# First batch of an attention and MLP kernel reordered: f32 staging of first heads, constants in two parts, PE transposes for the second batch, W1 ahead of most of W2

## Chip, cores, metric

One NeuronCore of a Trainium2 chip. The metric is device time of one execution in microseconds (us); most executions of one kernel agree to about 0.3%. Engines: PE = TensorE, DVE = VectorE, ACT = ScalarE, POOL = GpSimd, SP = SyncE. The clock of PE is read in two ways: the granted clock is a column of the profile, and the spacing of like matmuls shows the speed at which they ran.

## The reference

Grouped attention (8 batches, 16 q heads on 4 k/v heads, 384 positions, head size 64), then a residual MLP with an affine token mixer:

```python
scores = q @ k.T / sqrt(D);  attn = softmax(scores);  x = attn @ v   # x: [8, 384, 1024]
a1 = alpha1 * x + beta1
tok = einsum('ts,bsd->btd', w_tok, a1)
u = x + lam * tok
a2 = alpha2 * u + beta2
out = u + lam * (relu(a2 @ w_ch1) @ w_ch2)      # w_ch1: [1024, 4096], w_ch2: [4096, 1024]
```

Inputs are f32; the kernel works in bf16 and casts in the DMA where it can. W1 (w_ch1) does not stay on chip: each batch streams it again, 16 chunks through a ring of four. W2 stays.

## The kernel before

A batch has a side part (attention, tok, a2) and a main part (h = W1 product, ch = W2 product). The side part of batch b+1 is a list of small units that are interleaved with the matmuls of main(b). Batch 0 has no main part to hide behind: its side part is the prologue. A unit works on a pair of heads, p. A flip is a transpose; ident is the identity matrix with which PE transposes. The constants are alpha1 (g1), beta1 (h1), lam, alpha2 (al2) and beta2 (be2), spread over all partitions; "the chain" is DVE's work from its first reciprocal (softmax of the first pair) to the start of h.

```python
def load_q(b, i=0, n=Hq):              # cast to bf16 by POOL's DMA, pieces of one head row
    ...
    nc.gpsimd.dma_start(out=qrs[b][:, st, i:i + n], in_=by_st(q[b])[:, st, i:i + n])
...
def av_piece(p, hh):                   # one head of pair p
    ...                                # 9 matmuls
    if hh == 0:
        if p == 0 and first:           # constants folded once, whole width
            nc.vector.tensor_tensor(out=g1, in0=g1, in1=lam_t, op=MUL)
            nc.vector.tensor_tensor(out=h1, in0=h1, in1=lam_t, op=MUL)
        return
    ...                                # rinv, x (L205, L208), a1f = x * g1 (L211), a1 = a1f + h1 (L214)
def tok(p):
    ...                                # 9 matmuls; u (L224), a2f = u * al2 (L226), a2 = a2f + be2 (L229)
def a2_transpose(p):
    if not first:
        nc.sync.dma_start_transpose(...)   # batches 1 to 7
        return
    ...                                    # batch 0: PE and an ACT copy
...
# main(b), after W1 chunk c
load_w1(b * NCH + c + RING)
if b == 0 and c < 12:
    load_w2(1, c, NNT)
if b == 0 and c == 12:
    for i in range(3, 8):
        load_w2(1, i, 8)
...
# the program
load_k(0); load_q(0, 0, 8); make_identity(nc, ident)
... place_k(0); load_v(0); wtok_in; load_q(0, 8, 8)
for c in range(RING):
    load_w1(c)
load_w2(0, 0, 1)                       # the whole first half of W2, 4 MB in bf16
for i, f in enumerate(side(0)):
    f()
    ...                                # constants on ACT's queue after units 2 and 4, load_k(1) after 5
load_q(1); place_k(1); load_v(1); flip_k(1); flip_q(1)      # flips: DMA transposes
for b in range(B):
    us = side(b + 1) if b + 1 < B else []
    lead = 0.2 if b == 0 else 0.0
    for dt in main(b):                 # yields every 4 matmuls
        t += dt
        if done < len(us) and done * t_all * (0.95 - lead) < len(us) * (t - t_all * lead):
            us[done](); done += 1
```

The softmax here doesn't subtract the row's maximum and nothing guards it: scores larger than these inputs give would overflow.

## Time and profile before

| | us |
|---|---|
| time, median of 4 runs | 843.5 (842.17 to 843.87) |
| prologue, up to the first h matmul | 52.7 |
| batch 0 (h 61.4, ch 49.9) | 111.3 |
| batches 1 to 6, each | 98.1 |
| batch 7 (nothing beside it) and tail | 85.0 and 5.1 |

A stage begins at its first matmul.

### The profile page before, as it was taken

The numbers are of one execution on the slowest core, as the hardware profiler recorded it, in microseconds if no ns is written. First come the engines' busy times: TensorE is split into PE (matmuls) and PEld (weight loads), VectorE is DVE, ScalarE is ACT, GpSimd is POOL, SyncE is SP. The second block draws the span as 40 slices with busy tenths as digits, with TensorE's granted clock in tenths as the row PEclk, the third lists the DMA queues.
The fourth block names the chain that finished last, engine by engine and source line by source line (L and its number), as shares of the span: only waits on it lengthen the run. The fifth ranks groups of instructions, "written<-read, shape, count | busy, mean of one in ns | idle before, by whom it ended". The sixth has DMA issues, their size and how long they took to land.

```text
span 842.7 us, 13619 instructions
## 1 busy us (share of the span) xinstructions
PE 805.2 (96%) x5765; PEld 432.8 (51%) x5765; DVE 362.7 (43%) x737; ACT 210.7 (25%) x331; POOL 199.6 (24%) x246
## 2 busy tenths in 40 slices
PE   4776999999999999999999999999999999999997
PEld 2443544555545554555545554455545555455543
DVE  1741445534453444624445444544445345451111
ACT  5511432143113331043221331133320432101100
POOL 6473450022401232022500224012410221003100
PEclk9779999999999999999999999999999999999999
DMA  9999999699927999499975999279995999129811
GB/s 209 220 163 194 199 201 168 125 163 179 140 63 139 172 181 97 107 140 177 163 70 122 168 176 136 70 138 171 178 96 109 123 174 149 35 52 182 113 37 38
DMA packets 272045, 116.66 MB, mean 138 GB/s; under 512 B 121712, under 2 KB 265072, under 8 KB 271984
## 3 DMA queue, kind: packets, MB, share of 16 engines
q0 software_dynamic: 204000, 83.67, 86.5%
q1 hardware_dynamic: 67264, 29.50, 16.1%
q10 hardware_dynamic: 720, 2.62, 0.8%
q8 instruction: 45, 0.74, 0.3%
q14 instruction: 16, 0.13, 0.1%
HBM read 173.08 MB, written 12.58 MB: 220 GB/s over the span
## 4 chain that ended last, share of the span: by engine, by line
PE 88%; DMA 7%; DVE 3%; ACT 1%; issue 1%; POOL 0%; ACTq 0%; DVEq 0%; POOLq 0%
PE ch L331 40%; PE h L311 37%; DMA w<-in_moe_w_ch_dram 5%; PE sc L178 4%; PE av L196 4%; PE tok L221 4%; DMA h<-in_moe_beta_dram 1%; DMA q_raw<-in_q_dram 1%; DVE a2f L226 1%; DVE x L208 1%; DVE a1f L211 1%; ACT hT L316 0%; DVE x L224 0%; POOL q_raw L101 0%; DVE qT L170 0%
## 5 line engine op out<-in xcount | busy, mean ns | idle before, releaser
L311 PE MATMUL h<-a2T,w 128*128 128x384 bf16 x2048 | 361.6, 329 | 9.9 <-DMA w<-in_moe_w_ch_dram 9.0
L331 PE MATMUL ch<-w,hT 128*128 128x512 bf16 x1536 | 353.1, 379 | 0.0
L311 PEld LDWEIGHTS <-w 128*128 128x128 bf16 x2048 | 191.5, 98 | 149.7 <-issue 21.3
L125 POOL DMA_DIRECT2D w<-in_moe_w_ch_dram x128 | 112.4, 880 | 555.8 <-PE sc L178 273.3
L181 ACT ACTIVATE es<-sc 128x768 bf16<-128x768 f32 x192 | 145.3, 810 | 340.8 <-PE sc L178 340.6
L331 PEld LDWEIGHTS <-hT 128*128 128x128 bf16 x1536 | 142.3, 98 | 160.7 <-issue 9.2
L318 DVE TENSOR_SCALAR hT<-h 128x384 bf16<-128x384 f32 x128 | 71.2, 556 | 193.7 <-PE h L311 193.7
L316 ACT ACTIVATE hT<-h 128x384 bf16<-128x384 f32 x128 | 62.9, 492 | 233.4 <-PE h L311 233.4
L336 DVE TENSOR_TENSOR o<-ch,lam 128x512 f32<-128x512 f32 x48 | 33.1, 689 | 115.1 <-PE ch L331 115.1
L224 DVE TENSOR_TENSOR x<-tok,x 128x384 f32<-128x384 f32 x64 | 35.6, 556 | 80.5 <-PE tok L221 80.5
L196 PEld LDWEIGHTS <-es 128*128 128x128 bf16 x1152 | 52.5, 99 | 27.7 <-issue 6.5
L196 PE MATMUL av<-v,es 128*128 128x65 bf16 x1152 | 57.4, 195 | 4.5 <-DVE x L208 4.1
L178 PE MATMUL sc<-qT,kT 64*128 64x384 bf16 x384 | 51.7, 340 | 2.2 <-ACT es L181 1.3
L221 PE MATMUL tok<-a,wtokT 128*128 128x128 bf16 x576 | 44.2, 223 | 5.3 <-POOL a L214 2.8
L221 PEld LDWEIGHTS <-wtokT 128*128 128x128 bf16 x576 | 38.4, 100 | 16.9 <-issue 3.5
L208 DVE TENSOR_TENSOR x<-av,rinv 128x192 f32<-128x192 f32 x128 | 39.8, 352 | 2.2
L226 DVE TENSOR_TENSOR a2f<-x,al 128x384 f32<-128x384 f32 x64 | 37.4, 585 | 2.7
L211 DVE TENSOR_TENSOR a1f<-x,g 128x384 f32<-128x384 f32 x64 | 36.2, 566 | 2.7
L205 DVE RECIPROCAL rinv<-av 128x6 f32<-128x6 f32 x64 | 12.2, 191 | 55.7 <-PE av L196 55.7
L337 DVE TENSOR_TENSOR o<-o,x 128x512 f32<-128x512 f32 x48 | 33.2, 692 | 1.6
L229 DVE TENSOR_TENSOR a<-a2f,be 128x384 bf16<-128x384 f32 x57 | 31.8, 558 | 2.0
L214 DVE TENSOR_TENSOR a<-a1f,h 128x384 bf16<-128x384 f32 x57 | 31.8, 558 | 2.0
(32 smaller groups left out, 130.6 us busy)
## 6 DMA issues: line engine op xcount, KB each, us to landing
w<-in_moe_w_ch_dram POOLq DMA_DIRECT2D x133, 512.0 KB, 6.9
out_dram<-o SPq DMA_DIRECT2D x48, 256.0 KB, 2.2
q_raw<-in_q_dram POOLq DMA_DIRECT2D x21, 256.0 KB, 8.0
w<-in_moe_w_ch_dram POOLq DMA_DIRECT2D x1, 4096.0 KB, 39.8
kst<-in_k_dram SPq DMA_DIRECT2D x16, 192.0 KB, 3.1
v<-in_v_dram POOLq DMA_DIRECT2D x24, 64.0 KB, 7.8
w<-in_moe_w_ch_dram POOLq DMA_DIRECT2D x12, 128.0 KB, 9.9
a2T<-a SPq DMA_TRANSPOSE x56, 3.8
```

The source lines that it names most:

```text
L125: nc.gpsimd.dma_start(out=t, in_=w1src[:, :, c * CW * P:(c + 1) * CW * P])
L178: nc.tensor.matmul(out=sc[:, hh, :S].rearrange("p (st s) -> p st s", st=NST), lhsT=kT[r, sk, hk, :], rhs=qT[r, :, p, :], start=True, stop= ...
L181: nc.scalar.activation(out=e, in_=sc[:, :, :S], func=EXP, scale=scale_qk)
L196: nc.tensor.matmul(out=av[:, hh, sq, :], lhsT=ess[p, sk][:, hh, sq * P:(sq + 1) * P], rhs=vb[:, sk, hk, :], start=(sk == 0), stop=(sk == N ...
L208: nc.vector.tensor_tensor(out=x[:, :, c0:c0 + D], in0=av[:, hh, :, :D], in1=rinv[:, hh].to_broadcast([P, NST, D]), op=MUL)
L211: nc.vector.tensor_tensor(out=t, in0=x[:, :, cols(p)], in1=bc(g1, p), op=MUL)
L221: nc.tensor.matmul(out=ps[:, tt, :], lhsT=wtokT[:, st, tt * P:(tt + 1) * P], rhs=a1s[p][:, st, :], start=(st == 0), stop=(st == NST - 1))
L226: nc.vector.tensor_tensor(out=t, in0=u, in1=bc(al2, p), op=MUL)
L311: nc.tensor.matmul(out=ps[:, :S], lhsT=w1[:, dt, j * P:(j + 1) * P], rhs=a2T[:, dt, :], start=(dt == 0), stop=(dt == NDT - 1))
L316: nc.scalar.activation(out=hT[:, nt, :], in_=ps[:, :S], func=RELU)
L318: nc.vector.tensor_scalar_max(out=hT[:, nt, :], in0=ps[:, :S], scalar1=0.0)
L331: nc.tensor.matmul(out=ps, lhsT=hT[:, nt, ms * P:(ms + 1) * P], rhs=w2[:, nt, cs], start=(nt == 0), stop=(nt == NNT - 1))
```

## The change

Its intent is to shorten the prologue and to keep PE supplied in batch 0. Its parts: (1) k in separate halves, the first four q heads staged in f32 rows over ACT's queue, nine warming matmuls; (2) the constants in two column parts on two queues, issued early; (3) q, k and v of batch 1 loaded within the prologue; (4) PE transposes for k, q and a2 of batch 1, and DMA transposes for five of the eight a2 of batch 0; (5) half as much of W2 ahead of h, the rest between the chunks of W1; (6) batch 1's side work packed into h of batch 0.

```diff
+        pe_flip = b < 2
@@ av_piece
-                if p == 0 and first:
-                    ... g1 *= lam, h1 *= lam, whole width
+                if first and p in (0, 2):
+                    r = slice(0, 256) if p == 0 else slice(256, DM)
+                    ... the same on columns r
-            eng = nc.gpsimd if first and p < NP - 1 else nc.vector
+            eng = nc.gpsimd if first and p < NP - 2 else nc.vector     # both adds
@@ a2_transpose
-            if not first:
+            if not pe_flip or first and p < NP - 3:                    # by DMA
@@ side, batch 1: k and q transposes as units, tok and a2_transpose apart, and
+                    if pe_flip and j > 12:
+                        add(lambda: None)                              # 24 empty units
@@ main
-            if b == 0 and c < 12:
-                load_w2(1, c, NNT)
+            if b == 0 and 2 <= c < 12:
+                load_w2(*((0, 6 + c, 16) if c < 10 else (1, c - 10, 16)))
             if b == 0 and c == 12:
-                for i in range(3, 8):
+                for i in range(1, 8):
                     load_w2(1, i, 8)
@@ program
+        ... nine matmuls on a zeroed tile
         load_k(0)
-        load_q(0, 0, 8)
+        ... qst (f32) <- q[0, :4] on ACT's queue; load_q(0, range(1), 4)
         make_identity(nc, ident)
+        load_q(0, range(1, 3), 4)      # heads 4 to 15
+        ... cast of qst; columns 0:256 of g1, lam, h1 on ACT's queue
+        load_k(1); columns 256: of g1, lam, h1, then al2, be2 on SP's queue
         ... load_v(0), wtok_in, load_w1(0..3)
-        load_w2(0, 0, 1)
+        loads = {8: [(load_w2, 0, 0, 2)], 19: [(load_q, 1, [0]), (load_q, 1, [1])],
+                 25: [(load_q, 1, [2]), (load_v, 1, [0])], 37: [(load_v, 1, [1])], 43: [(load_v, 1, [2])]}
-        load_q(1); place_k(1); load_v(1); flip_k(1); flip_q(1)
+        place_k(1, 0); place_k(1, 1)   # on DVE and ACT now
-            lead = 0.2 if b == 0 else 0.0             # span 0.95 - lead
+            lead, span = (0.04, 0.82) if b == 0 else (0, 0.95)
```

More of the change, by code (lines that the diff above doesn't have):

```diff
@@ L68 @@
     hT = const.tile([P, NNT, S], bf, tag="hT", name="hT")
+    g1, h1, lam_t, al2, be2 = (const.tile([P, DM], f32, tag=n, name=n)
+                               for n in ("g1", "h1", "lam", "al2", "be2"))
     kT = const.tile([P, NST, Hkv, P], bf, tag="kT", name="kT")
@@ L84, in load_k, with place_k @@
             ks[b].append(t)
-    def place_k(b):
-        k2s[b] = t = sb.tile([P, NST, Hkv, 2, D], bf, tag="k2", name="k2", bufs=1)
-        copies = (nc.vector.tensor_copy, nc.scalar.copy) if b == 0 else [nc.gpsimd.tensor_copy] * 2
-        for i, src in enumerate(ks.pop(b)):
-            for a in range(2):
-                copies[a](out=t[:, :, 2 * i:2 * i + 2, a, :], in_=src.rearrange("p h st d -> p st h d"))
+    def place_k(b, i):
+        if i == 0:
+            k2s[b] = sb.tile([P, NST, Hkv, 2, D], bf, tag="k2", name="k2", bufs=1)
+        copies = (nc.vector.tensor_copy, nc.scalar.copy) if b < 2 else [nc.gpsimd.tensor_copy] * 2
+        for a in range(2):
+            copies[a](out=k2s[b][:, :, 2 * i:2 * i + 2, a, :], in_=ks[b][i].rearrange("p h st d -> p st h d"))
     def load_v(b, sts=range(NST)):
@@ L95, in load_v, with load_q @@
             nc.gpsimd.dma_start(out=vt[b % 2][:, st, :, :D], in_=by_st(v[b])[:, st])
-    def load_q(b, i=0, n=Hq):
+    def load_q(b, sts=range(NST), i=0):
         if b not in qrs:
             qrs[b] = sb.tile([P, NST, Hq, D], bf, tag="q_raw", name="q_raw", bufs=1)
-        for st in range(NST):
-            nc.gpsimd.dma_start(out=qrs[b][:, st, i:i + n], in_=by_st(q[b])[:, st, i:i + n])
+        for st in sts:
+            nc.gpsimd.dma_start(out=qrs[b][:, st, i:], in_=by_st(q[b])[:, st, i:])
     def flip_k(b):
@@ L109, in flip_q, with bcast @@
                                     in_=qrs[b].rearrange("p st h d -> p (st h d)"))
-    def bcast(ap, name):
-        t = const.tile([P, DM], f32, tag=name, name=name)
-        src = bass.AP(tensor=ap.tensor, offset=ap.offset, ap=[[0, P]] + [list(x) for x in ap.ap])
-        nc.scalar.dma_start(out=t, in_=src)
-        return t
+    def bcast(eng, t, ap, lo, hi):
+        src = bass.AP(tensor=ap.tensor, offset=ap.offset + lo, ap=[[0, P], [1, hi - lo]])
+        eng.dma_start(out=t[:, lo:hi], in_=src)
     w1src = moe_w_ch1.rearrange("(dt di) nf -> di dt nf", di=P)
@@ L166, in q_transpose @@
                 nc.tensor.matmul(out=ps[:, i, :],
-                                 lhsT=qrs[0][:, i % NST, h:h + 2, :].rearrange("p h d -> p (h d)"),
+                                 lhsT=qrs[b][:, i % NST, h:h + 2, :].rearrange("p h d -> p (h d)"),
                                  rhs=ident, is_transpose=True, start=(i == 0),
@@ L199, in av_piece @@
             if hh == 0:
-                if p == 0 and first:
-                    nc.vector.tensor_tensor(out=g1, in0=g1, in1=lam_t, op=MUL)
-                    nc.vector.tensor_tensor(out=h1, in0=h1, in1=lam_t, op=MUL)
+                if first and p in (0, 2):
+                    r = slice(0, 256) if p == 0 else slice(256, DM)
+                    nc.vector.tensor_tensor(out=g1[:, r], in0=g1[:, r], in1=lam_t[:, r], op=MUL)
+                    nc.vector.tensor_tensor(out=h1[:, r], in0=h1[:, r], in1=lam_t[:, r], op=MUL)
                 return
@@ L209, in av_piece @@
                                         in1=rinv[:, hh].to_broadcast([P, NST, D]), op=MUL)
-            t = sb.tile([P, NST, P], f32, tag="tmp", name="a1f", bufs=3)
+            t = sb.tile([P, NST, P], f32, tag="tmp", name="a1f", bufs=4)
             nc.vector.tensor_tensor(out=t, in0=x[:, :, cols(p)], in1=bc(g1, p), op=MUL)
             a1s[p] = sb.tile([P, NST, P], bf, tag="a1", name="a1", bufs=2)
-            eng = nc.gpsimd if first and p < NP - 1 else nc.vector
+            eng = nc.gpsimd if first and p < NP - 2 else nc.vector
             eng.tensor_tensor(out=a1s[p], in0=t, in1=bc(h1, p), op=ADD)
@@ L224, in tok @@
             nc.vector.tensor_tensor(out=u, in0=ps, in1=u, op=ADD)
-            t = sb.tile([P, NST, P], f32, tag="tmp", name="a2f", bufs=3)
+            t = sb.tile([P, NST, P], f32, tag="tmp", name="a2f", bufs=4)
             nc.vector.tensor_tensor(out=t, in0=u, in1=bc(al2, p), op=MUL)
             a2s[p] = sb.tile([P, NST, P], bf, tag="a2", name="a2", bufs=3)
-            eng = nc.gpsimd if first and p < NP - 1 else nc.vector
+            eng = nc.gpsimd if first and p < NP - 2 else nc.vector
             eng.tensor_tensor(out=a2s[p], in0=t, in1=bc(be2, p), op=ADD)
         def a2_transpose(p):
-            if not first:
+            if not pe_flip or first and p < NP - 3:
                 nc.sync.dma_start_transpose(
@@ L263, in side @@
         if not first:
-            done = -1
-            for j in range(NP * NST // 2 + 3):
+            if pe_flip:
+                add(k_transpose, 0)
+                add(q_transpose, 0)
+                add(k_transpose, 2)
+                add(q_transpose, 1)
+            for j in range(NP * NST // 2 + 4):
                 if 2 * j < NP * NST:
                     add(scores2, j)
+                if pe_flip and j in (1, 4):
+                    add(q_transpose, 2 + j // 4)
                 for p in range(NP):
-                    if (NST * p + NST - 1) // 2 == j - 1:
+                    last = (NST * p + NST - 1) // 2
+                    if last == j - 1:
                         add(av_piece, p, 0)
                         add(av_piece, p, 1)
-                    if (NST * p + NST - 1) // 2 == j - 3:
-                        add(tok_flip, p)
+                    if last == j - 3:
+                        add(tok if pe_flip else tok_flip, p)
+                    if pe_flip and last == j - 4:
+                        add(a2_transpose, p)
+                    if pe_flip and j > 12:
+                        add(lambda: None)
             return us
@@ L276, in side @@
         add(q_transpose, 0)
-        for p in range(NP + 5):
-            if p < NP:
-                add(scores, p, 0)
-                if p == 1:
-                    add(k_transpose, 2)
-                add(scores, p, 1)
-            if 0 < p <= NP:
+        for p in range(NP):
+            add(scores, p, 0)
+            if p == 1:
+                add(k_transpose, 2)
+            add(scores, p, 1)
+            if p < 3:
+                add(q_transpose, p + 1)
+            if p > 0:
                 add(av_piece, p - 1, 0)
-            if p == 3:
+            if p == 2:
                 add(wtok_transpose)
-            if 0 <= p - 3 < NP:
-                add(tok, p - 3)
-            if p < NP:
-                add(scores, p, 2)
-            if p % 2 == 0 and p + 2 < NP:
-                add(q_transpose, p // 2 + 1)
-            if 0 <= p - 5 < NP:
-                add(a2_transpose, p - 5)
-            if 0 < p <= NP:
-                add(av_piece, p - 1, 1)
+            if p > 2:
+                add(tok_flip if p < NP - 1 else tok, p - 3)
+            add(scores, p, 2)
+            if p > 0:
+                add(av_piece, p - 1, 1)
+        for p in range(NP - 3, NP):
+            if p == NP - 2:
+                add(av_piece, NP - 1, 0)
+                add(av_piece, NP - 1, 1)
+            add(tok, p)
+        for p in range(NP - 4, NP):
+            add(a2_transpose, p)
         return us
@@ L334, in main @@
                         yield T_C
-                o = sb.tile([P, 512], f32, tag="o", name="o", bufs=2)
+                o = sb.tile([P, 512], f32, tag="tmp", name="o", bufs=4)
                 nc.vector.tensor_tensor(out=o, in0=ps, in1=lam_t[:, cs], op=MUL)
@@ L344 @@
     with tc.manual_schedule(engines=order):
+        nc.vector.memset(wtokT, 0.0)
+        warm = psum.tile([P, 512], f32, tag="mm", name="warm", bufs=2)
+        for _ in range(9):
+            nc.tensor.matmul(out=warm[:, :S], lhsT=wtokT[:, 0, :P], rhs=wtokT[:, 1, :],
+                             start=True, stop=True)
         load_k(0)
-        load_q(0, 0, 8)
+        qst = sb.tile([P, NST, DM], f32, tag="x", name="qst", bufs=2)
+        qst = qst[:, 0, :G * NST * D].rearrange("p (h st d) -> p h st d", h=G, st=NST)
+        nc.scalar.dma_start(out=qst, in_=q[0, :G].rearrange("h (p st) d -> p h st d", st=NST))
+        load_q(0, range(1), G)
         make_identity(nc, ident)
@@ L349 @@
             nc.vector.memset(t[:, :, :, D:], 1.0)
-        place_k(0)
+        load_q(0, range(1, NST), G)
+        place_k(0, 0)
+        for h, cp in ((0, nc.vector.tensor_copy), (2, nc.scalar.copy)):
+            cp(out=qrs[0][:, :, h:h + 2, :], in_=qst[:, h:h + 2].rearrange("p h st d -> p st h d"))
+        for t, ap in ((g1, moe_alpha1), (lam_t, moe_lam), (h1, moe_beta1)):
+            bcast(nc.scalar, t, ap, 0, 256)
+        place_k(0, 1)
+        load_k(1)
+        for t, ap in ((g1, moe_alpha1), (lam_t, moe_lam), (h1, moe_beta1)):
+            bcast(nc.sync, t, ap, 256, DM)
+        bcast(nc.sync, al2, moe_alpha2, 0, DM)
+        bcast(nc.sync, be2, moe_beta2, 0, DM)
         load_v(0)
@@ L353 @@
         nc.gpsimd.dma_start(out=wtok_in, in_=moe_w_tok.rearrange("(p tt) s -> p tt s", tt=NST))
-        load_q(0, 8, 8)
         for c in range(RING):
             load_w1(c)
-        load_w2(0, 0, 1)
+        loads = {8: [(load_w2, 0, 0, 2)], 19: [(load_q, 1, [0]), (load_q, 1, [1])],
+                 25: [(load_q, 1, [2]), (load_v, 1, [0])], 37: [(load_v, 1, [1])], 43: [(load_v, 1, [2])]}
         for i, f in enumerate(side(0)):
             f()
-            if i == 2:
-                g1 = bcast(moe_alpha1, "g1")
-                lam_t = bcast(moe_lam, "lam")
-                h1 = bcast(moe_beta1, "h1")
-            if i == 4:
-                al2 = bcast(moe_alpha2, "al2")
-                be2 = bcast(moe_beta2, "be2")
-            if i == 5:
-                load_k(1)
-        load_q(1)
-        place_k(1)
-        load_v(1)
-        flip_k(1)
-        flip_q(1)
+            for g, *a in loads.get(i, []):
+                g(*a)
+        place_k(1, 0)
+        place_k(1, 1)
         for b in range(B):
@@ L381 @@
                 t += dt
-                if done < len(us) and done * t_all * (0.95 - lead) < len(us) * (t - t_all * lead):
+                if done < len(us) and done * t_all * span < len(us) * (t - t_all * lead):
                     us[done]()
@@ L386 @@
                     loaded = True
-                    place_k(b + 2)
+                    place_k(b + 2, 0)
+                    place_k(b + 2, 1)
                     load_q(b + 2)
```

## The prediction

> **What bounds the kernel now.** I read the page's slices first, then stretches cut at the first and last matmul of each stage (h is line 311, ch is line 331), then the order of time on DVE, POOL and PE in the first 115 us.
>
> The slices of the page:
>
> ```profile
> PE   4776999999999999999999999999999999999997
> PEclk9779999999999999999999999999999999999999
> DMA  9999999699927999499975999279995999129811
> GB/s 209 220 163 194 199 201 168 125 163 179 140 63 139 172 181 97 107 140 177 163 70 122 168 176 136 70 138 171 178 96 109 123 174 149 35 52 182 113 37 38
> ```
>
> One slice is 21 us. PE is full from the fifth slice on, so only the first four or five slices can give anything back. The stretches (start:end, then busy us of PE, PEld, DVE, ACT, POOL, then clock, DMA share, GB/s):
>
> ```profile
> 0.00:53.00 53.00, 30.20 (x334) 20.46 (x335) 29.72 (x65) 23.43 (x35) 29.94 (x37) 0.85 1.28 208
> 53.00:114.00 61.00, 53.38 (x356) 28.43 (x355) 17.33 (x36) 17.65 (x30) 29.27 (x41) 0.93 1.48 187
> 114.00:164.00 50.00, 50.00 (x358) 24.77 (x357) 26.63 (x54) 8.53 (x12) 8.34 (x11) 1.00 1.14 162
> 164.00:262.00 98.00, 97.85 (x713) 52.69 (x712) 45.06 (x92) 25.55 (x40) 21.50 (x26) 1.00 1.03 137
> ```
>
> These four are the prologue (attention of batch 0), h of batch 0, ch of batch 0, and batch 1. From the first matmuls of each stage: h of batch 0 starts at 52.74, of batch 1 at 164.01, and every later batch lasts 98.09; the last, which has no attention beside it, lasts 85.0, then 5 us of tail. So attention costs 98.09 - 85.0 = 13.1 us of PE a batch when hidden, and batch 0 at PE's pace would last about 98 us where it took 111.3. The prologue and batch 0 hold all that can be won.
>
> Prologue, DVE in order of time (start, length, ..., idle before and what ended it):
>
> ```profile
> 14.46 0.56 DVE L159 COPY kT<-tp 128x768 bf16<-128x768 bf16 x1 [0.89 <-PE tp L157]
> 20.15 1.22 DVE L201 TENSOR_TENSOR g<-g,lam 128x1024 f32<-128x1024 f32 x1 [5.13 <-DMA lam<-in_moe_lam_dram]
> 21.75 1.22 DVE L202 TENSOR_TENSOR h<-h,lam 128x1024 f32<-128x1024 f32 x1 [0.38 <-DMA h<-in_moe_beta_dram]
> 22.89 0.19 DVE L205 RECIPROCAL rinv<-av 128x6 f32<-128x6 f32 x1
> ...
> 41.40 0.69 DVE L211 TENSOR_TENSOR a1f<-x,g 128x384 f32<-128x384 f32 x1
> 42.01 0.55 DVE L224 TENSOR_TENSOR x<-tok,x 128x384 f32<-128x384 f32 x1
> 42.66 0.98 DVE L226 TENSOR_TENSOR a2f<-x,al 128x384 f32<-128x384 f32 x1
> ```
>
> DVE waits 5 us for the broadcast constants although the first head pair's av was finished at about 16.5. After 22.89 DVE works with little idle, 3.1 us a pair, up to 52.4: the prologue is first constants, then DVE.
>
> h of batch 0, PE in order of time, and the POOL queue that issues the weights:
>
> ```profile
> 52.74 13.18 PE L311 MATMUL h<-a2T,w 128*128 128x384 bf16 x64
> 67.28 2.77 PE L311 MATMUL h<-a2T,w 128*128 128x384 bf16 x16 [1.37 <-DMA w<-in_moe_w_ch_dram]
> 72.45 2.77 PE L311 MATMUL h<-a2T,w 128*128 128x384 bf16 x16 [2.39 <-DMA w<-in_moe_w_ch_dram]
> ```
>
> ```profile
> 51.10 3.49 POOL L101 DMA_DIRECT2D q_raw<-in_q_dram  x3
> 54.55 1.88 POOL L91 CAST k<-kst 128x384 bf16<-128x384 f32 x4
> 56.36 2.25 POOL L95 DMA_DIRECT2D v<-in_v_dram  x3
> 58.58 0.92 POOL L125 DMA_DIRECT2D w<-in_moe_w_ch_dram  x1
> ```
>
> The four W1 chunks in the ring are used up, then PE waits for each chunk. Batch 1's q, casts of k and v stand ahead of the first refill in the POOL queue, and the DMA transposes of batch 1 run beside it:
>
> ```profile
> kT<-k SPq DMA_TRANSPOSE x1, 7.6
> qT<-q_raw SPq DMA_TRANSPOSE x1, 18.8
> ```
>
> **What the Trainium skill says.** "TensorE: Matmul & The Clock Gate", Part 1: the array runs at half clock until some 3.4 us of sustained work, and goes back after an idle window. The trace agrees: h matmuls start 0.32 us apart from 52.74 to 58.0 and 0.16 us apart after; the granted clock was half up to 17 us, from 23.9 to 34.1, 47.8 to 58.0 and 78.5 to 81.9. "DMA: Bandwidth & Descriptors", Issuing engines are not separate DMA queues: queues on other engines save only issue time, so constants on two queues get no more bandwidth, only their place in the order. Same page, Specifications: pieces under 512 B are below line rate. The trace agrees: the first 12 us, mostly 128-byte pieces of q and v, moved 151 GB/s, the next 18 us 262. "Perfetto Trace Analysis", Roofline: one core is bounded by its 16 DMA engines at about 435 GB/s; the casting weight loads here write 195 to 200 GB/s, which is 390 to 400 read.
>
> **The change part by part.**
>
> (1) Start. Four q heads come in f32 in long rows; ident is made after one q issue and not three. PE waited 4.8 us for ident, and about as long for k, so k's transpose moves little; the first scores move from 10.3 to about 8.5. But the next q group (second transpose) now waits for 12-head loads, issued 2.9 to 5.0 and, at the 5 us that the last 8-head load took after its issue, landing at 10.5 to 11. The first av pieces so stay near 14 to 15, the nine warming matmuls (9 x 0.32 us, while nothing else can run) saving about 1 us in between by the clock.
>
> (2) Constants. The first 256 columns (3 x 128 KB instead of 3 x 512 KB) are issued at about 5.5 instead of 10.9 and should be there by 12 to 13. The first pair's DVE chain then starts when its av ends, at about 15.5 instead of 22.89: 7.4 us earlier.
>
> (3) The DVE chain from there. Before it took 52.74 - 22.89 = 29.85. Added: the 768-column products, 2 x 0.93 = 1.9 (1.22 x 0.75), inside the chain now; pair 6's two adds from POOL to DVE, 2 x 0.56 = 1.1. Removed: of some 3.5 us of idle (0.57, 0.57, 1.02, 0.83, 0.55) perhaps 2, as wtok comes one pair earlier and tok flips leave PE. Five a2 transposes by DMA cost DVE nothing. Chain 30.9, so h starts at 15.5 + 30.9 = 46.4, against 52.74.
>
> (4) Batch 0. PE work is 85.0 + 13.1, and for the flips of batch 1: six groups of six transposes at 0.058 us (0.35 a group) plus eight of three at 0.17, together 3.5. Sum 101.6. The side work is packed early: 50 real pieces followed by 24 empty ones in a list of 74, starting at 4% of the batch with a span of 82%, so about 41 of the 50 fall in h. h should last 43.8 + 0.85 x 16.6 = 58, ch 41.2 + 2.5 = 44.
>
> (5) DMA in h. Until the last chunk, 12 chunks x 1.05 MB and W2 of 4.7 MB and k of 0.4 MB are read: 17.7 MB at 0.395 MB/us = 45 us, plus 3 to the first refill and 2 of latency = 50; PE comes to chunk 15 at 15/16 x 58 = 54. So it is just hidden. Before, chunk 15 was reached 58 us after h's start. What must land before h (about 10 MB written, at the 208 GB/s of the prologue 48 us) is about done at its start.
>
> (6) I add 1.9 for the half clock at h's start (2.6 was lost before) and evictions held up by denser DVE work. Batch 0: 103.5 instead of 111.3, 7.8 won. Batches 1 to 7 keep their times; the shared "tmp" buffers touch no wait of PE.
>
> Sum: 6.3 + 7.8 = 14.1, time 843.84 - 14.1 = 829.8, say 830.0.
>
> **The rivals.** (A) DVE is the prologue's bound whatever starts it: the transposes of wtok and the shared transpose bank hold PE and DVE in step, the chain grows to 34, h starts at 50. For it: DVE was 8.4 and 9.2 busy of 10 us from 30 to 50, and gets more work. Time about 834. (B) The DMA engines stay the bound of h: they were at nine tenths throughout, the whole of W2's second quarter now falls into h, and loads moved ahead of h are still the same bytes. Then h lasts 62, ch 44, and the time is about 832 to 835. Against it: the two large flips go, and the POOL queue is clear. (C) Everything overlaps: x starts at 15, no idle in the chain, h at 44, batch 0 in 102: time about 826. (D) Dense side work holds up the evictions of h or the transposes' one bank, batch 0 takes 107: time about 834. PE waits of this kind hardly show in batches 1 to 6, but there the density is half as much.
>
> **Range and chances.** The errors of prologue and batch 0 are each about 3 us and only weakly linked: 824.0 to 837.0 for 8 in 10. Over 2% needs 16.9 us, that is rival C: 0.27. Slower by 2% has no mechanism in the profile: 0.01. Within 2%: 0.72.
>
> **What would show each step right or wrong.** DVE's first reciprocal at 15 to 16.5, not after a wait for lam; the second q group's transposes ending a wait for q at 10 to 11; h of batch 0 from about 46, 58 long with no DMA wait over 1 us, ch about 44; batches 1 to 6 at 98.1; POOL issuing the first refill right after chunk 0. I am wrong if h starts after 49 (A), if PE waits for w in h by more than 3 us (B), or if the gain is over 17 us (C).

## The result

835.09 us (median of 4 runs, 832.76 to 836.01) against 843.5. The ratio of the fast runs is 0.9899, 95% interval 0.9876 to 0.9922; a ratio here is the record's, formed from the fast runs of both kernels in one session, so not quite the ratio of the medians. The change wins 8.4 us, 1%: within the range, and 5.1 us slower than the predicted time.

The stretches of the changed kernel (start:end, length, busy us of PE, PEld, DVE, ACT, POOL, clock, DMA share, GB/s): h of batch 0, ch of batch 0, batch 1.

```profile
52.00:111.60 59.60, 59.51 (x530) 35.50 (x527) 32.20 (x71) 28.74 (x48) 24.13 (x31) 0.98 1.24 175
111.60:155.40 43.80, 43.80 (x253) 21.12 (x250) 15.06 (x28) 1.44 (x3) 10.10 (x13) 1.00 1.30 191
155.40:253.40 98.00, 97.85 (x713) 52.65 (x712) 45.08 (x92) 25.54 (x40) 21.50 (x26) 1.00 1.11 137
```

From the stages' first matmuls in the trace:

| stage | before | predicted | after |
|---|---|---|---|
| first reciprocal on DVE | 22.89 | 15.5 | 18.35 |
| from there to h of batch 0 | 29.85 | 30.9 | 33.7 |
| start of h of batch 0 | 52.74 | 46.4 | 52.05 |
| h, ch of batch 0 | 61.4, 49.9 | 58, 44 | 59.6, 43.8 |
| batch 0 | 111.3 | 103.5 | 103.3 |
| batches 1 to 6, each | 98.1 | 98.1 | 98.1 |

Batch 0 is the whole of the gain. The spans differ by 9.4 us: 0.7 at the start of h, 8.0 in batch 0, and 0.8 in batch 7, where before two waits for W1 came to 1.4 us; the changed kernel's second profile has 85.2 there and not 84.2, against 85.0 before, so I count that as chance.

Batch 0 in PE's waits, the kernel before first (engine, line, what was waited for, us, times, longest):

```profile
PE h L311 <- DMA w<-in_moe_w_ch_dram: 7.5, 7, 2.4
```

and all of the changed kernel's between 52 and 156 us:

```profile
PE tp L241 <- DVE a L231: 1.4, 1, 1.4
```

The one wait left is at the very end of the prologue; the weights wait is gone. Two things were won in batch 0 and one was paid. PE stood idle for 7.6 us of it before and for 0.1 after. It ran 8.7 us of it at half clock before (52.7 to 58.0 and, after the waits for W1, 78.5 to 81.9) and 2.7 after; that is worth up to 3.0 us, an estimate (half of 6.0). The transposes now on PE cost some 3.5 us by the prediction's sum. This makes 7.0 of the 8.0.

The prologue of the changed kernel, PE in order of time:

```profile
11.23 0.61 PE L167 MATMUL tp<-ident,q_raw 128*128 128x128 bf16 x4 [1.76 <-DMA q_raw<-in_q_dram]
...
16.73 0.55 PE L197 MATMUL av<-v,es 128*128 128x65 bf16 x7 [1.81 <-DMA v<-in_v_dram]
...
51.75 0.50 PE L241 MATMUL tp<-ident,a 128*128 128x128 bf16 x3 [1.35 <-DVE a L231]
52.05 5.41 PE L327 MATMUL h<-a2T,w 128*128 128x384 bf16 x24
```

and DVE:

```profile
18.35 0.20 DVE L207 RECIPROCAL rinv<-av 128x6 f32<-128x6 f32 x1 [2.29 <-PE av L197]
...
24.49 0.95 DVE L203 TENSOR_TENSOR g<-g,lam 128x768 f32<-128x768 f32 x1
25.36 1.75 DVE L204 TENSOR_TENSOR h<-h,lam 128x768 f32<-128x768 f32 x1
...
33.66 1.81 DVE L228 TENSOR_TENSOR a2f<-x,al 128x384 f32<-128x384 f32 x1
...
51.14 0.56 DVE L231 TENSOR_TENSOR a<-a2f,be 128x384 bf16<-128x384 f32 x1 [0.92 <-DMA a2T<-a]
```

The constants no longer hold DVE; v does, and PE meets q first. After the first pair the chain is longer than before by the 768-column products, by slower multiplies (one a2f took 1.81 us, where the kernel before had 0.56 to 0.99), and by a wait for the buffer of an a2 that a DMA is still transposing. The slow multiplies have POOL's adds beside them: the one of 1.81 us ended at 35.47, 0.42 us after an add on POOL (34.04 to 35.05), the one of 0.98 at 37.53 also 0.42 us after its add (37.10 to 38.09), as if each had stood still until the add was over. No run tests this alone.

### The profile page after: what moved, and what is told of

The parts are those of the page before. It is cut to its first block, busy times and chain, and to the rows that moved or that the text cites. A ratio compares the mean times of both kernels' runs of the same rounds, so it can differ in the third digit from the quotient of the medians.

```text
span 833.3 us, 13722 instructions
## 1 busy us (share of the span) xinstructions
PE 807.3 (97%) x5819; PEld 436.9 (52%) x5819; DVE 371.5 (45%) x751; ACT 213.2 (26%) x337; POOL 195.9 (24%) x237
## 3 DMA queue, kind: packets, MB, share of 16 engines
q1 hardware_dynamic: 62064, 30.26, 15.5%
## 4 chain that ended last, share of the span: by engine, by line
issue 61%; POOL 16%; PE 13%; DMA 7%; DVE 2%; POOLq 0%; ACT 0%; DVEq 0%; ACTq 0%
POOL w L125 11%; PE h L327 5%; PE ch L347 5%; DMA w<-in_moe_w_ch_dram 4%; POOL q_raw L103 2%; POOL v L97 2%; DMA v<-in_v_dram 1%; POOL k L93 1%; DMA a2T<-a 1%; PE sc L179 1%; PE av L197 1%; DVE a2f L228 1%; PE tok L223 1%; DVE a1f L213 0%; DVE x L210 0%
## 5 line engine op out<-in xcount | busy, mean ns | idle before, releaser
L125 POOL DMA_DIRECT2D w<-in_moe_w_ch_dram x128 | 112.6, 880 | 555.5 <-PE sc L179 274.0
L353 DVE TENSOR_TENSOR o<-o,x 128x512 f32<-128x512 f32 x48 | 33.2, 692 | 1.6
```

The source lines that it names most:

```text
L125: nc.gpsimd.dma_start(out=t, in_=w1src[:, :, c * CW * P:(c + 1) * CW * P])
```

## The experiments

All start from the changed kernel, except the one that says otherwise. The table gathers them; times are medians, each beside runs of the kernel before, stages are from one profile each.

| run | time | ratio to before (95%) | first reciprocal | h starts | h, ch | batch 0 |
|---|---|---|---|---|---|---|
| changed kernel | 835.09 | 0.990 (0.988 to 0.992) | 18.35 | 52.05 | 59.6, 43.8 | 103.3 |
| k0_again, same | 834.79 | 0.991 (0.988 to 0.994) | 17.54 | 50.27 | 59.4, 43.8 | 103.2 |
| k1_late_q1 | 835.01 | 0.991 (0.988 to 0.993) | 16.94 | 50.12 | 59.5, 43.8 | 103.2 |
| k3_dma_flips | 839.64 | 0.997 (0.993 to 1.002) | 16.95 | 50.72 | 64.3, 43.3 | 107.6 |
| k5_spacing | 845.18 | 1.002 (0.998 to 1.005) | 20.18 | 54.77 | 57.9, 54.8 | 112.6 |
| k5b_spacing | 839.53 | 0.994 (0.993 to 0.996) | 17.01 | 51.05 | 56.3, 50.6 | 106.9 |
| k4_w2_first | 843.36 | 0.999 (0.997 to 1.001) | 17.59 | 50.76 | 67.8, 43.8 | 111.5 |
| k11, before + packing | 847.6 | 1.004 (1.002 to 1.006) | 24.00 | 53.85 | 71.8, 43.0 | 114.8 |
| k2_whole_consts | 837.67 | 0.992 (0.991 to 0.994) | 20.08 | 52.85 | 59.7, 43.8 | 103.5 |
| k10_old_start | 842.82 | 1.000 (0.998 to 1.002) | 25.96 | 58.93 | 60.6, 43.8 | 104.3 |
| k6_v_first | 838.24 | 0.994 (0.992 to 0.996) | 22.78 | 56.21 | 61.0, 43.8 | 104.8 |
| k9_three | 836.7 | 0.993 (0.991 to 0.994) | 18.83 | 51.67 | 59.3, 43.8 | 103.0 |
| k12_best | 840.02 | 0.996 (0.994 to 0.998) | 14.02 | 57.30 | 59.9, 43.8 | 103.7 |

### The same kernel again

> The changed kernel once more, for the spread of its stages from run to run. All theories: span 831 to 835, first matmul of h of batch 0 at 51 to 53 us (52.05 in the first profile), batch 0 in 102.5 to 104.5 us (103.3 before this run), about 0.99 of the kernel before. A start of h that moves by over 1.5 us would mean that single profiles can't settle effects of 1 us in the prologue.

It holds, and it warns: h began 1.8 us earlier than in the first profile of the same kernel. PE waited 3.6 us for q and not for v, where the first profile had 1.8 and 1.8. The prologue of this kernel scatters by 2 us in these two profiles, batch 0 by 0.2. Three runs below have the same prologue (k3, k5, k5b), and k5_spacing began h at 54.77, so the scatter is 4.5 us. Single profiles thus settle batch 0, and in the prologue only effects of over 4.5 us, or those whose own wait is in the lines.

### Batch 0: which part wins the 8 us

Theory: h of batch 0 was at the pace of the weight loads; the gain needs loads in time and side work packed where PE would wait. Rivals: one part alone is enough.

```diff
# k1_late_q1
-        loads = {8: [...], 19: [...], 25: [...], 37: [...], 43: [...]}
+        loads = {8: [(load_w2, 0, 0, 2)]}
...
+        load_q(1); load_v(1)          # after side(0)
```

> q and v of batch 1 are loaded after the first batch's attention, as in the kernel before, not within it. Theory (DVE chain of the prologue is stretched by what POOL does beside it, and early loads are what keeps h of batch 0 free of waits): h starts 1 to 2 us earlier (50 to 51), but batch 0 grows by 5 to 9 us, because PE reaches the transposes of batch 1's q before it has landed and the first W1 refill is issued later; time 838 to 843. Rival 1 (early loading does nothing for batch 0, only the order of W2 does): batch 0 stays at 103 to 104, time 833 to 835. Rival 2 (POOL's issues don't disturb DVE): h still starts at 52.

The first rival is right about batch 0: 103.2, no wait. POOL had done its adds by 44 us and issued q and v of batch 1 from 43.8 to 49.5. From issue to landing, the three loads of q took in the changed kernel (issued from 26.2 to 31.1) and in this run:

```profile
DMA to landing us min/median/max: 22.6/24.5/25.1
```

```profile
DMA to landing us min/median/max: 5.9/6.6/7.2
```

The last of them landed at 53.7 in the one and at 53.3 in the other, since 2 MB of W2 stand ahead of them in POOL's queue in both and landed at 47.3 and 47.7. PE met q at 58.4 and 56.4. So the early issue moved no landing.

On DVE the effect is small: the eight a2f multiplies took, in the changed kernel's second profile and in this run (line, operation, count, busy us, mean ns, idle before):

```profile
L228 DVE TENSOR_TENSOR a2f<-x,al 128x384 f32<-128x384 f32 x8 | 7.0, 874 | 0.7
```

```profile
L228 DVE TENSOR_TENSOR a2f<-x,al 128x384 f32<-128x384 f32 x8 | 6.2, 774 | 0.7
```

With 0.3 on a1f that is 1.1 us, and the chain does not show it: 33.2 us here, 33.7 and 32.7 in the changed kernel. My expected 5 to 9 us were wrong: early issue of q and v of batch 1 wins nothing behind the same part of W2.

```diff
# k3_dma_flips: batch 1's k, q and a2 by DMA transpose, empty units in place of theirs
-        pe_flip = b < 2
+        pe_flip = b < 1
...
+        flip_k(1); flip_q(1)          # after place_k(1, 1)
```

> The flips of batch 1 (k, q, a2) go back to DMA transposes; their units are replaced by empty ones, so the spacing stays. Theory (transposes by DMA slow the weight loads and land late, so PE pays about 3.5 us for transposes and saves more in waits): batch 0 takes 106 to 112 us instead of 103.3, with PE waiting for qT or for w over 4 us in h; time 838 to 843. Rival (h of batch 0 has DMA time to spare after the reordering of W2, and PE only pays for the transposes): batch 0 takes 100 us, time about 831.

Batch 0 took 107.6, as the theory had it. PE's waits from 50 to 160 us:

```profile
PE h L326 <- DMA w<-in_moe_w_ch_dram: 3.4, 4, 1.2
PE sc L180 <- DMA qT<-q_raw: 3.0, 1, 3.0
```

PE saves its own transposes (I had put them at 3.5 us) and batch 0 still is 4.3 us longer: transposes on PE are the cheaper ones here. What PE waits for is transfers, 6.4 us, and they are slower: the first two refills of W1 landed 8.1 and 9.1 us after their issue, in the changed kernel 5.7 us each.

```diff
# k5_spacing
-            lead, span = (0.04, 0.82) if b == 0 else (0, 0.95)
+            lead, span = (0.2, 0.75) if b == 0 else (0, 0.95)
-                    if pe_flip and j > 12:          # no empty units
-                        add(lambda: None)
# k5b_spacing: the same lead and span, but
-                    if pe_flip and j > 12:
+                    if pe_flip and j > 12 and p < 3:
```

> Side work of batch 1 spread as before: lead 0.2, span 0.75 and no empty units, all else as changed. Theory (h of batch 0 is at the pace of the weight loads at about 50 us, so work packed into it is free, and the same work in ch is not): h of batch 0 takes 52 to 54 us with 2 to 4 us of waits for w, ch 50 to 51, batch 0 104.5 to 106, time 836 to 838. Rival (PE is the only bound of batch 0 once the loads are reordered, the spacing shifts work and wins nothing): h about 50, ch about 53, batch 0 103 to 104, time 834 to 835.

It went beyond the theory, 112.6, and for a reason of its own: without empty units the last a2 transposes stand right behind their tok, and PE waited 3.5 us for DVE there. Also its h began with the clock at half for 4.3 us. So I repeated it with nine empty units:

> Mend of the run with the old spacing: there, dropping all empty units put the a2 transposes straight behind their tok and PE waited 3.5 us for DVE, which is none of the spacing's doing. Now lead 0.2 and span 0.75 with three empty units before each late group (9 instead of 24). Theory (h of batch 0 is at the weight loads' pace, work packed into it is free): those 3.5 us of waits go, waits for w of 4 to 6 us in h stay, batch 0 takes 107 to 110 us against 103.2, time 839 to 842. Rival (the loss of the first spacing run was only the waits of the a2 transposes and the clock): batch 0 103 to 105, time 834 to 836.

106.9: 3.7 us longer than the changed kernel, just under the expected 107 to 110. The split shows why. Against the packed kernel, h is 3 us shorter and ch 7 us longer: of 7 us of side work moved out of h, h gives back only 3. PE's idle time in batch 0 is 3.1 us in this profile (2.1 of it waits for W1) against 0.1, which is most of the 3.7. The rival (no loss but the slip) falls.

```diff
# k4_w2_first
-8: [(load_w2, 0, 0, 2)]
+8: [(load_w2, 0, 0, 1)]
...                                    # and the slices within h as in the kernel before
```

> W2 in its old order: its whole first half issued behind the first four W1 chunks, twelve slices of 128 KB within h, the rest after; all else as changed. Theory (2 MB more ahead of batch 1's q and v in the one queue of POOL delay them by about 10 us and PE meets its q transposes early in h): PE waits 3 to 8 us for q_raw or v in h of batch 0, or for w, batch 0 takes 106 to 111 us, time 838 to 843. Rival (the bytes before the last W1 chunk are nearly the same in both orders, so nothing is won by it): batch 0 103 to 104, time 834 to 835.5.

The theory holds, with 111.5 a little over its range: the order of W2 alone gives back all of batch 0's gain. PE in order of time:

```profile
60.72 0.29 PE L167 MATMUL tp<-ident,q_raw 128*128 128x128 bf16 x1 [3.60 <-DMA q_raw<-in_q_dram]
62.60 0.29 PE L167 MATMUL tp<-ident,q_raw 128*128 128x128 bf16 x1 [1.59 <-DMA q_raw<-in_q_dram]
64.27 0.61 PE L167 MATMUL tp<-ident,q_raw 128*128 128x128 bf16 x4 [1.38 <-DMA q_raw<-in_q_dram]
```

What counts is what stands ahead of batch 1's q in POOL's one queue. With 2 MB more of W2 there, W2 landed at 58.2 and not at 47.3, and the last load of q at 64.2 and not at 53.7:

```profile
DMA to landing us min/median/max: 33.9/35.2/35.9
```

That is the delay of 10 us that I had expected. The packed unit that has no q yet stops h as well: no h matmul ran between 57.1 and 64.67. The clock fell to half from 60.2 to 67.1. The three waits are 6.6 us; PE's busy time at half clock in batch 0 is 6.0 us against 2.7, worth some 1.7 us more, an estimate.

```diff
# k11_before_packed: the kernel before, with the packing alone
-            lead = 0.2 if b == 0 else 0.0
+            lead, span = (0.04, 0.82) if b == 0 else (0, 0.95)
+                    if b == 1 and j > 11:
+                        add(lambda: None)
```

> The kernel before with the early packing alone (lead 0.04, span 0.82, 24 empty units at the end), no other part of the change. Theory (packing wins only with batch 1's q and k there and flipped in time): PE stands before batch 1's first scores until the DMA transpose of q lands, 8 to 15 us, or waits as long for w; batch 0 takes 109 to 116 us against 111.3, time 842 to 850. Rival (packing alone is the gain of batch 0): batch 0 takes 103 to 106, time 836 to 839.

The theory holds: slower than the kernel before, with one wait of 11.7 us:

```profile
72.06 0.82 PE L178 MATMUL sc<-qT,kT 64*128 64x384 bf16 x4 [11.65 <-DMA qT<-q_raw]
```

So batch 0's 8 us belong to no single part: undoing the packing loses 3.7, the PE flips 4.3, W2's order 8.2; packing alone loses 3.5. They are not additive.

### The prologue: why it won almost nothing

```diff
# k2_whole_consts: g1, lam, h1 whole on ACT's queue after unit 2, al2, be2 after 4, load_k(1) after 5
-                if first and p in (0, 2):
+                if first and p == 0:          # products whole
```

> The constants come whole on ACT's queue after the first scores as before, their products are taken whole before the first pair, and batch 1's k is loaded after them; all else as changed. Theory (the first pair starts earlier by the two parts, but DVE then has the rest of the products in its chain, so only part of the start is kept): first reciprocal at 21 to 24 instead of 17 to 18.4, the chain from there 2 to 3 us shorter than 33, h of batch 0 starts at 52.5 to 55 against 50.3 to 52; time 836 to 838.5. Rival (DVE's total work decides, the start does not): h starts where it does in the changed kernel, 50 to 52, time 834 to 835.

First reciprocal at 20.1, 1.7 and 2.5 us later than in the changed kernel's two profiles; h at 52.85, 0.8 to 2.6 later than the changed kernel's two profiles. The chain from the first reciprocal was 32.8, not 2 to 3 us shorter than 33, although no product is in it: a2f took 7.6 us and waits for tok and wtok filled in. Both figures lie within the scatter of the prologue (k5_spacing, with the parts: 20.18 and 54.77). In time the intervals overlap. So the parts win about 1 us or nothing; this run doesn't tell which. But it shows what the early constants cost. With them issued from 8.9 us on and not from 5.2, the three loads of v, issued at the same times, took to land (the changed kernel first, then this run):

```profile
DMA to landing us min/median/max: 8.1/8.8/10.2
```

```profile
DMA to landing us min/median/max: 6.0/6.2/6.2
```

The last of them landed at 12.7 and not at 16.7 (15.3 in the second profile).

```diff
# k10_old_start: no qst, no warming, q as in the kernel before; the constants' parts stay
+        load_q(0, range(NST), 0, 8)    # ahead of ident
...
+        load_q(0, range(NST), 8, Hq)   # behind wtok, ahead of W1
```

> From the changed kernel: q loads as before (heads 0 to 7 cast by three DMAs ahead of ident, the rest behind wtok), no f32 stage of q and no warming matmuls; the parts of the constants stay. Theory (the staging moves the first scores from 10.3 to 8.3 but the next q group and v are later by as much, so it wins nothing at the first pair): first reciprocal at 16.5 to 18.5, h starts at 50 to 52.5, time 834 to 836. Rival (the staging gives the 2 us that the first scores show): first reciprocal at 19 to 20.5, h at 52.5 to 54, time 836.5 to 838.

Both were wrong, by far: first reciprocal at 25.96, h at 58.93, and all of the gain is gone. PE in order of time:

```profile
9.72 0.29 PE L167 MATMUL tp<-ident,q_raw 128*128 128x128 bf16 x1 [3.31 <-DMA q_raw<-in_q_dram]
12.14 0.61 PE L167 MATMUL tp<-ident,q_raw 128*128 128x128 bf16 x4 [2.13 <-DMA q_raw<-in_q_dram]
...
22.09 0.29 PE L167 MATMUL tp<-ident,q_raw 128*128 128x128 bf16 x1 [4.90 <-DMA q_raw<-in_q_dram]
```

In the kernel before, the same three loads had landed by 9.0 and the second three never stopped PE; the constants were issued from 10.9 on. Here the constants are issued from 3.4 us on, the first three loads landed by 12.1 and the second three by 23.7. The stage in f32 is thus not worth the 2 us of the first scores: with early constants the new start is worth 7 us or more (h at 58.93 against 50.27 and 52.05). With late constants it shows nothing: h began at 52.85 in k2 and at 52.74 in the kernel before. The new start is three things, though, the stage, the warming matmuls and the order of q's loads, and k10 undoes all three; that the stage alone does it is not shown.

Three runs tried to cure what the lines of the changed kernel name.

```diff
# k6_v_first: v issued first, transposes of q's later heads one pair later
+        load_v(0)
         make_identity(nc, ident)
...
-            if p < 3:
-                add(q_transpose, p + 1)
+            if 0 < p < 4:
+                add(q_transpose, p)
# k9_three: k6 and
+                    eng = nc.vector if p == 0 else nc.gpsimd       # products of columns 256: on POOL
-            if not pe_flip or first and p < NP - 3:
+            if not pe_flip:                                        # a2 flips of batch 0 all on PE
```

> From the changed kernel: v of batch 0 is issued before q's heads 4 to 15, and the transposes of those heads come one pair later, so PE meets neither v nor q before they are there. Theory (the first pair starts late because v and q stand in line): the waits of PE for q_raw (1.8 and 3.6 us) and v (1.8 us) in the first 20 us go, the first reciprocal comes at 14 to 16 instead of 17 to 18.4, h starts 1.5 to 3 us earlier, at 48 to 50; batch 0 stays at 103.3; time 832 to 833.5. Rival (DVE's work is the bound and idle gaps open elsewhere): first reciprocal earlier, h still at 50 to 52, time 834.5 to 835.5.

> A version that should beat both: v first as in the run beside it, the products of the last 768 columns of the constants on POOL behind its first add instead of on DVE, and all a2 flips of batch 0 on PE (two pairs later, as in the kernel before) instead of five by DMA. Theory (what DVE does and waits for after the first pair is the prologue): the chain from the first reciprocal to h is 29 to 31 us instead of 33 (2.7 of products, 0.2 to 1.6 of waiting for a flip's DMA), first reciprocal at 14 to 16, h starts at 44 to 47, batch 0 103 to 104, time 828 to 831. Rival (POOL's products slow DVE and delay the adds of pairs 1 and 2 by as much as they take off): h at 48 to 50, time 832 to 834.

Both carry a slip of mine: DVE's memset of the ones in v's tile now came behind v's load in program order, and held DVE:

```profile
7.50 0.52 DVE L93 CAST k<-kst 128x384 bf16<-128x384 f32 x1 [6.03 <-DMA v<-in_v_dram]
```

(k9; k's cast had run at 4.25 in the changed kernel.) So k6 does not test its idea; it also waited 5.5 us for q. k9 shows something in spite of it: its chain was 32.8 us, no shorter, although the wait for the DMA's buffer and DVE's products were gone. POOL took 1.8 us for each product, its add of pair 1 came at 26.2 instead of 24.7, and two a2f multiplies beside it took 1.7 and 1.8 us.

```diff
# k12_best: memset first; v first; av of pair 1 ahead of q's second group; qT and wtok copies on ACT;
#           a2 flips on PE; q and v of batch 1 after side(0)
```

> A mend of the three-cure run, where DVE's memset of v's ones had come behind v's load and held DVE up until 7.5 us (a slip of the edit, not of the idea). Now the memset is ahead, v is issued first, PE meets q's later heads only where their scores need them (both av pieces of pair 1 ahead of them), the copies of those transposes and of wtok go to ACT, a2 flips of batch 0 are all on PE two pairs later, and batch 1's q and v are issued after POOL's adds as in the late-q1 run. The products stay on DVE. Theory (waits for v and q before the first pair, and DVE's work after it, set the prologue): first reciprocal at 13.5 to 16, chain 30 to 32 us, h starts at 45 to 48, batch 0 103 to 105, time 829 to 832 against about 835 of the changed kernel. Rival (other waits fill the gap, or late q1 now makes PE wait in h): h at 49 to 52 or batch 0 over 106, time 834 to 838.

The first reciprocal came at 14.0, as expected, and h at 57.3, the rival's way and worse. PE:

```profile
11.54 0.68 PE L198 MATMUL av<-v,es 128*128 128x65 bf16 x9
...
15.98 0.29 PE L167 MATMUL tp<-ident,q_raw 128*128 128x128 bf16 x1 [1.26 <-DMA q_raw<-in_q_dram]
23.05 0.61 PE L167 MATMUL tp<-ident,q_raw 128*128 128x128 bf16 x4 [6.78 <-DMA q_raw<-in_q_dram]
```

With v first, q's later heads were issued from 4.75 to 7.8 and the last landed at 23: DVE then had nothing for 9.2 us. Against the changed kernel's first profile v landed 9.5 us earlier (7.2) and q 11.8 us later. No run beat the changed kernel.

## Why the prediction was right in its range and 5 us too fast

- **Batch 0 (step 4) was right**, 103.5 against 103.3 and 103.2, with h 58 and ch 44 against 59.5 and 43.8. The reason was right as well: the packed side work hides behind the loads (undone: 106.9), with flips on PE (undone: 107.6) and the queue clear ahead of batch 1's q (undone: 111.5). Step 5's count of bytes was a poor guide to the last: the old order of W2 has nearly the same bytes before the last chunk and loses 8.2. There it is the queue ahead of q that counts. That early issue of q and v of batch 1 is needed, as I expected before k1, is wrong.
- **The step that failed is the prologue (steps 1 to 3)**: predicted 6.3 us, measured 0.7 and, in the second profile, 2.5. The prediction gave this part an error of about 3 us, and it named a start of h after 49 as a sign of being wrong; h began at 52.05. That the time fell in the range is due to the range's width and to batch 0, not to this part. I took the first av pieces to "stay near 14 to 15". They ended at 17.3 and 18.3, because I let the loads of q delay only q (landed at 11.2, near the forecast 10.5 to 11): v stands behind them in the same queue, landed at 16.7, and the early constants run beside both (without them it landed at 12.7, k2). That term is 2.9 us of the miss in the first profile. The 1 us from the warming matmuls did not come there either: the groups of six transposes at 5.38 and 6.88 took 0.80 us, as the one at 4.77 in the kernel before; in the second profile the first two took 0.56 and 0.49, and the wait for q took it up.
- **The chain** was mis-sized by 2.8 us (30.9 against 33.7). By its terms: the products took 2.7, not 1.9; the adds of pair 6 took the 1.1 that I had; a1f and a2f grew by 0.8 each, which I had at nothing; a copy of 0.5 fell ahead of the chain; the idle time went down by 1.0 (3.5 to 2.5), not 2. With these, 29.85 + 2.7 + 1.1 + 1.6 - 0.5 - 1.0 = 33.75.
- **Rivals**: A's figures (h at 50, a chain of 34, 834 us) came nearest; its mechanism, that DVE is the bound whatever starts it, is not shown (in k12 DVE stood idle for 9.2 us and h began at 57.3). B (the loads stay the bound of h), C (h at 44) and D (batch 0 in 107) did not come.
- **Slips in the prediction** that change little: 843.84 - 14.1 is 829.7, not 829.8; 1.22 x 0.75 is 0.92, not 0.93; and the clock column shows no half clock before 23.9, the half clock "up to 17 us" is seen in the spacing of matmuls alone.
- **Left open**: what sets the end of the prologue. Removing single delays (k1, k9) did not shorten the chain by what they took away; k10 and k12 show that PE's order against the landing of q can put off its end by 5 us or more. I have no run in which everything lands in time, so I can't say what DVE alone would need.

## What to carry to other kernels

When a start is short of transfers, moving one load earlier moves others later: list what is in flight beside it, and place the consumers in PE's order by landing times, since one missing tile stopped all that stood behind it on PE (6.6 us in k4, 11.7 in k11). Work that can be placed freely is worth most in the stage that waits for memory, but only if its own inputs are sure to be there. Size a chain on a busy engine with durations taken beside the neighbour that it will have, not from a quiet stretch.

## What the Trainium skill lacked or had wrong

- "DMA: Bandwidth & Descriptors", Issuing engines are not separate DMA queues, says that queues on other engines save only issue time. The section says nothing of how long one load then takes, and the page, which tells elsewhere how the engines take turns between queues, has no figure for it. Three 192 KB loads of 128-byte pieces on POOL's queue, issued within 3.7 us in the changed kernel's first profile and within 3.1 in k12, landed by 11.2 us in the first and only by 23 in the second, beside constants on the queues of SP and ACT in both, with v's pieces ahead of them in the second.
- "GPSIMD Engine Reference", Specifications, says that its SBUF interfaces are shared with VectorE and that DVE instructions with two SBUF inputs contend. It gives no size there; other pages of the skill say more of this sharing, so this is no gap of the skill as a whole. Here a 128x384 multiply of two SBUF inputs took 0.56 us alone, mostly 0.9 to 1.06 beside a POOL add, and up to 1.81; the two whose ends are given above ended 0.42 us after the add. The addition of tok, with one input in PSUM, stayed at 0.54 to 0.56 us.
- "TensorE: Matmul & The Clock Gate", Part 4, gives some 275 ns for one transpose in a kernel and no spacing of transposes (the page has one for plain matmuls). Here one shows 219 ns at full clock but six in a row start 0.056 us apart (0.107 at half clock), so that a group of six costs PE some 0.34 us.
